# Values of two token chunks as one seven-product pair, with deadlines in the order model, in a tuned attention and feed-forward kernel

## The chip, the cores and the metric

The kernel runs on one core of a Trainium2 chip. The metric is the device time of that core in microseconds, the median of the timed runs. Runs of one version here lie up to 0.5% apart, so two versions are compared in rounds: both run by turns on the same chip. Where a **ratio** is given, it is the mean time of one kernel's fast runs over the mean of the other's in the same rounds, with a 95% interval; it is therefore not quite the ratio of the medians quoted beside it. One execution of each kernel is also recorded by the hardware profiler. All stage times below are from such traces.

## The reference

```python
x = A_x                                             # 2048 tokens x 1024, bf16
g = sigmoid((x * gate_w).sum(-1, keepdims=True))    # one gate for each token
a = attention(x, wqkv) @ wo                         # 32 heads, each token sees 8 tokens, 2 apart, itself included
b = (gelu(x @ w_gate) * (x @ w_up)) @ w_down        # inner width 3584
out = g * a + (1 - g) * b
```

The weights are `wqkv` (1024 x 3072), `wo` (1024 x 1024), `w_gate` and `w_up` (1024 x 3584) and `w_down` (3584 x 1024).

## The kernel before

The tokens are cut into four chunks of 512. Chunks 0 and 1 form a first pair, chunks 2 and 3 a second. The work of a pair is: projections to Q, K and V; up and gate products; down products, in which the attention output (with `wo`) and the feed-forward output (with `w_down`) are handled in one contraction.

Most of these products already use a **seven-product form**. A product of two matrices that are each cut into 2 x 2 quarters needs eight quarter products. Seven are enough if some of them take sums and differences of the quarters ("forms") as operands. TensorE saves one matmul in eight, and VectorE pays: it builds the forms of the weights and of x, and adds up partial results. In the kernel before, the up and gate products, the down products and the projections of chunks 2 and 3 are done so. The projections of chunks 0 and 1 are plain: for each chunk and each of Q, K and V, 8 output tiles x 8 contraction tiles = 64 matmuls of 128 x 512.

The order of instructions on every engine is fixed while the program is built. A small model holds a clock for each engine and a set of streams (generators of operations). It picks, again and again, the operation whose modelled start plus the bias of its stream is least:

```python
    def run(self, streams):
        ...
        while live:
            best = None
            for s in live:
                op = s[2] if isinstance(s[2], Op) else s[2]()
                t = None if op is None else self._start(op)
                if t is not None and (best is None or t + s[0] < best[0]):
                    best = (t + s[0], t, s, op)
            ...
            _, t, s, op = best
            self._emit(op, t)          # the engine order is now fixed
            s[2] = next(s[1], None)
    ...
    w.run([(0.0, main()), (0.0, loads()), (0.0, late_x()), (0.1, wforms()), (0.1, x_forms()), (0.1, qkv_forms()),
           (0.15, preps()), (0.3, attention()), (0.5, scores())])
```

`main` holds TensorE's work. `scores` and `attention` are the sliding-window attention on VectorE. `wforms` are the weight forms of up and gate. `preps` are the weight forms of the down products, prepared once and stored in DRAM: nine groups of four VectorE operations, each group loaded with 1 MB. The loads come in this order:

```python
    def loads():
        yield from load_qkv(0, 0)      # Q's weights, by eight rows of tiles, into ring buffers
        yield load_prep(0)
        yield from load_qkv(0, 1)      # K's
        yield Op("SP", ..., lambda: [nc.sync.dma_start(out=vbuf[...], in_=qkv_src(2, ...)) for hf in range(2)], ...)  # V's
        yield from load_x(1, [])
        yield load_prep(2)
        yield from load_block(0, 0)    # up and gate weights
        ...
    # main(), after the transposes of chunk 0
        yield from qkv_outer(0)        # Q of chunk 0
        yield from qkv(0, 1)
        yield from qkv(0, 2)           # V of chunk 0, 64 matmuls
        yield from gate(0)
        yield from halo(1)
        for which in range(3):
            yield from qkv(1, which)   # the third is V of chunk 1, 64 matmuls
            ...
        yield from gate(1)
```

Of the kernel before, what the change touches and what calls it, by code (L numbers as in the profile page):

```python
# [30 lines left out]
class Op:  # L31


    def __init__(self, eng, cost, fn, deps=(), key=None, table=None, pre=None, lag=0.0, tail=0.08, kind=None):
        self.eng, self.cost, self.fn, self.deps, self.key = eng, cost, fn, deps, key
        self.table, self.pre, self.lag, self.tail = table, pre, lag, tail
        self.kind = kind
        self.end = None


class Weave:
# [6 lines left out]
    RATE = 340e3  # L48

    def __init__(self, nc, tc):  # L50
        self.nc, self.tc = nc, tc
        self.clk = {e: 0.0 for e in ("PE", "DVE", "ACT", "POOL", "SP")}
        self.pipe = 0.0
        self.table = None
        self.done = {}
        self.last = {}
        self.log = []
        self.names = []

# [9 lines left out]
    def _start(self, op):  # L69
# [9 lines left out]
        t = self.clk[op.eng]  # L79
        for d in deps:  # L80
            t = max(t, d.end + (0.04 if d.eng == op.eng else self.LAT + op.lag))
        return t

    def _emit(self, op, t):
# [4 lines left out]
        if op.eng in ("SP", "POOL"):  # L89
            nbytes, issue = op.cost  # L90
            self.clk[op.eng] = t + issue
# [8 lines left out]
        for ins in self.nc.cur_bb.bb.instructions[n0:]:  # L100
# [4 lines left out]
            if prev is not None:  # L105
                self.tc.add_manual_dep(ins, prev, mybir.DependencyInfo(mybir.DependencyClass.NoSync,
                                                                      mybir.DependencyReason.DATA),
                                       reason="engine order")
            self.last[eng] = ins.name
# [5 lines left out]
    def run(self, streams):  # L115
# [5 lines left out]
        while live:  # L121
            best = None
            for s in live:
                op = s[2] if isinstance(s[2], Op) else s[2]()
                t = None if op is None else self._start(op)
                if t is not None and (best is None or t + s[0] < best[0]):
                    best = (t + s[0], t, s, op)
# [9 lines left out]
def kernel(  # L137
# [51 lines left out]
    hT = persist.tile([P, 2 * NST, FT, P], BF16)  # L189
# [8 lines left out]
    XB = 9  # L198
    ring = persist.tile([P, NG, GR], BF16)
# [3 lines left out]
    ident = hT[:, NST + 1, 0, :]  # L203
# [10 lines left out]
    def hflat(j, f0, n):  # L214
        return hT[:, j, f0:f0 + n, :].rearrange("p f s -> p (f s)")
# [57 lines left out]
    for j in range(NST):  # L273
        (nc.sync if j % 2 == 0 else nc.scalar).dma_start(out=hflat(j, 0, 8), in_=x[j * P:(j + 1) * P, :])
    warm = hT[:, NST, 0:SC // P, :].rearrange("p a b -> p (a b)")
# [19 lines left out]
    vbuf = hT[:, :, 0:NT, :].rearrange("p k f n -> p k (f n)")  # L295
    NPREP = FH + NTH
    NSTG = 3
    def stage(i):
        f0 = FT - 4 * (i + 1)
        return hT[:, :, f0:f0 + 4, :].rearrange("p (a b) f s -> p a b (f s)", b=2)  # L300
# [9 lines left out]
    def load_x(c, deps):  # L310
        deps = deps + ([[("acct", 1)], [("att", 0)]][c - 2] if c > 1 else [])
# [58 lines left out]
    def loads():  # L370
        yield from load_qkv(0, 0)
        yield load_prep(0)
        yield from load_qkv(0, 1)
# [3 lines left out]
        yield from load_x(1, [])  # L377
        yield load_prep(2)
# [7 lines left out]
        for sup in range(NSUP):  # L386
            c0 = 2 * sup
            more = sup + 1 < NSUP
            if more:
                yield from load_down(c0)  # L390
                for which in range(3):
                    yield from load_qkv(c0 + 2, which, [k for i in range(KH) for k in (i, i + KH)],
                                        [("wq", c0 + 2, which - 1, 3, KH - 1)] if which else [])
                yield from load_down(c0 + 1, [("wq", c0 + 2, 2, 3, KH - 1)])
# [6 lines left out]
    def preps():  # L401
        for i0 in range(0, NPREP, 2):
# [5 lines left out]
            f0 = dve(t, lambda: V(out=b11, in0=b12, in1=b11, op=ALU.subtract), [("prep", i0)], lag=1.0)  # L408
            yield f0
            yield dve(t, lambda: V(out=b12, in0=b22, in1=b12, op=ALU.subtract))  # L410
            f1 = dve(t, lambda: V(out=b22, in0=b22, in1=b11, op=ALU.subtract), [f0])
            yield f1
            last = dve(t, lambda: V(out=b21, in0=b21, in1=b22, op=ALU.subtract), [f1])
# [12 lines left out]
    def wforms():  # L426
        t = tt(GR)
        for b in range(NBLK):
            ops = []
            for f, x_, y_, op in ((0, "U21", "A22", ALU.add), (2, "A11", "U21", ALU.subtract), (1, 0, "A11", ALU.subtract),  # L430
# [5 lines left out]
                o = dve(t, go, [("w", 0, b, x_), ("w", 0, b, y_)], key=("w", 0, b, f), lag=0.5, pre=ring_pre)  # L436
# [28 lines left out]
    def qkv_w(c, which, kt):  # L465
        if c < 2 and which == 2:
            return vbuf[:, kt, :]
# [6 lines left out]
    def halo(c):  # L474
        for z, n in ((kT, 1), (vT, 2)):
            src = [("qkv", c - 1, n, t) for t in range(NT)]
            yield act(0.2, lambda z=z: nc.scalar.copy(out=z[c][:, :, 0:HALO], in_=z[c - 1][:, :, SC:SC + HALO]),
                      src + ([("acct", 2 * c - 3), ("att", c - 2)] if c > 2 else []),
                      key=("halo", c, n))

    def qkv(c, which):
        src = 0 if c < 2 else c
        shared = c < 2 and which == 2
        dw = [("wqkv", 0, 2)] if shared else [("wqkv", src, which, kt) for kt in range(KT)]
# [13 lines left out]
        if c != 0 and not shared:  # L498
            for kt in range(KT):
                ring_give(("wqkv", src, which, kt), o)  # L500

    def qkv_outer(c):
        taken = [bank_take() for t in range(NT)]
        for kt in range(KT):
# [11 lines left out]
            if c:  # L516
                ring_give(("wqkv", c, 0, kt), o)
# [10 lines left out]

    def qkv_forms():
        for sup in range(1, NSUP):  # L530
            c = 2 * sup
            t = tt(D // 2)
            for which in range(3):
                def g3(key):
                    return ring[:, held[key], :].rearrange("p (m t) -> p m t", t=NT)

                def raw(kt, hi, which=which, c=c):
                    return g3(("wqkv", c, which, kt))[:, :, KH * hi:KH * hi + KH]
# [5 lines left out]
                for f in range(4):  # L544
                    for kt in range(KH):
                        if True:
# [9 lines left out]
                            dep = [("wqkv", c, which, kt), ("wqkv", c, which, kt + KH)]  # L556
                            if f in (1, 2):
                                dep.append(("wq", c, which, 0, kt))
                            elif f == 3:
                                dep.append(("wq", c, which, 1, kt))  # L560
                            yield dve(t, go, dep, key=("wq", c, which, f, kt), lag=0.5,
                                      pre=ring_pre if (f != 2 and kt % 2 == 0) else None)

    def q_tmp(t):
        return hT[:, t // 2, FT - NT + KH * (t % 2):FT - NT + KH * (t % 2 + 1), :].rearrange("p f s -> p (f s)")

    def v_tmp(t):
        v = hT[:, t, FH:FH + KH, :] if t < 2 else hT[:, 2 + (t - 2) // 3, NTH + KH * ((t - 2) % 3):NTH + KH * ((t - 2) % 3 + 1), :]
        return v.rearrange("p f s -> p (f s)")

    def v_move(c):
# [3 lines left out]
        def fn():  # L575
            nc.sync.dma_start(out=dst[:, 0:2], in_=hT[:, 0:2, FH:FH + KH, :].rearrange("p j f s -> p j (f s)"))
            for j in range(2):
                nc.sync.dma_start(out=dst[:, 2 + 3 * j:5 + 3 * j],
# [711 lines left out]
```

## Time and profile before

| | |
|---|---|
| median of 4 timed runs | 730.04 us (729.64 to 730.49) |
| the profiled execution | 728.63 us, so 1 us faster than any of the timed ones |
| matmuls | 3397 |

The first part of the page of the kernel before gives busy time, share of the span and number of instructions for each engine:

```profile
PE 721.2 (99%) x3397; PEld 355.8 (49%) x3397; DVE 593.9 (82%) x874; ACT 316.0 (43%) x533; POOL 72.4 (10%) x128
```

The second part cuts the span into 40 slices of 18 us; each digit is the busy share in tenths. VectorE (DVE) is at nine tenths or more in most slices to 260 us:

```profile
DVE  2769999999999989986999979989999995793200
DMA  9985868998887969964128999857576656999992
```

The chain of waits of the kernel before, in order of time, shows what the end time hangs on. The columns are the start, the length (us), then engine, tile, line and number of instructions. L472 are the plain projections, L973 the up and gate products, L608 the seven-product projections of chunks 2 and 3:

```profile
49.90 13.97 PE ps L472 x64
...
64.05 27.78 PE ps L472 x128
...
92.37 5.30 PE ps L973 x24
...
97.84 63.99 PE ps L973 x296
...
161.85 97.76 PE ps L973 x452
...
317.57 72.67 PE ps L608 x336
```

The last line gives the price of a matmul in a dense stream: 72.67 us / 336 = 216.3 ns.

PE's waits in the kernel before are tiny. The columns are the tile, the line, what it waited for, then total us, how often, longest:

```profile
PE ps L278 <- DVE hT L276: 1.2, 1, 1.2
PE ps L1215 <- DMA hT<-in_A_x_dram: 0.6, 1, 0.6
PE ps L472 <- DVE lend L1222: 0.2, 1, 0.2
```

All three are at the start, before or in the first projections. There is also a table of stretches of the same kernel. After the length come the busy time and count of each engine, then TensorE's clock, the DMA share (the mean busy share of the core's 16 DMA engines; the view can show a little over 1) and GB/s.

```profile
core 0: us, PE busy (x) PEld busy (x) DVE busy (x) ACT busy (x) POOL busy (x), PEclk, DMA share, GB/s
92.37:130.00 37.63, 37.63 (x183) 16.98 (x183) 36.73 (x60) 22.03 (x39) 13.17 (x21) 1.00 0.78 252
130.00:165.00 35.00, 34.98 (x163) 15.79 (x162) 32.48 (x50) 21.91 (x37) 12.91 (x21) 1.00 1.08 350
```

From 92 to 130 us VectorE is busy for 36.73 of 37.63 us (98%), and from 130 to 165 us the DMA share is at its top, 1.08 at 350 GB/s. TensorE is not the only engine without slack there.

### The profile page before, as it was taken

The page shows a single profiled execution, that of the slowest core. Times are in us where ns is not written, and L with a number is a line of the kernel's source. Part 1 is how long each engine was busy: PE and PEld are TensorE (multiplying, and loading weights), DVE is VectorE, ACT ScalarE, POOL GpSimd, SP SyncE. Part 2 cuts the span into 40 slices and gives each one's busy share as a digit, 9 for nine tenths or more (in the row PEclk, how much of TensorE's full clock was granted, in tenths as well). Part 3 has the DMA queues.
Part 4 walks back from the last instruction along what each step waited for, and adds up shares of the span by engine and source line. Part 5 has one row for each costly group of instructions (what it writes and reads, how often), then busy time and mean ns, then how long its engine had stood idle before and what let it go on. Part 6 is the DMA issues. An engine that isn't in the chain of part 4 may idle for free.

```text
span 726.9 us, 9989 instructions
## 1 busy us (share of the span) xinstructions
PE 721.2 (99%) x3397; PEld 355.8 (49%) x3397; DVE 593.9 (82%) x874; ACT 316.0 (43%) x533; POOL 72.4 (10%) x128
## 2 busy tenths in 40 slices
PE   8999999999999999999999999999999999999998
PEld 6666644444444444456665444444444444444443
DVE  2769999999999989986999979989999995793200
ACT  2333455576555561045443114585558556210110
POOL 1131224443212000000000000000000000001000
PEclk9999999999999999999999999999999999999999
DMA  9985868998887969964128999857576656999992
GB/s 305 273 264 157 236 209 293 319 367 274 214 215 203 232 197 339 329 193 128 47 87 282 353 315 358 250 156 183 149 184 160 173 150 171 306 333 333 328 308 99
DMA packets 185043, 172.12 MB, mean 237 GB/s; under 512 B 56480, under 2 KB 145568, under 8 KB 184992
## 3 DMA queue, kind: packets, MB, share of 16 engines
q1 hardware_dynamic: 176160, 143.69, 67.7%
q0 software_dynamic: 8544, 27.27, 10.2%
q8 instruction: 26, 0.43, 0.2%
q10 hardware_dynamic: 288, 0.52, 0.2%
q14 instruction: 25, 0.20, 0.1%
HBM read 129.50 MB, written 28.31 MB: 217 GB/s over the span
## 4 chain that ended last, share of the span: by engine, by line
PE 98%; ACT 1%; DMA 0%; issue 0%; DVE 0%; ACTq 0%
PE ps L973 46%; PE ps L1120 30%; PE ps L472 11%; PE ps L608 10%; DMA hT<-in_A_x_dram 0%; PE ps L1215 0%; PE ps L716 0%; ACT L1061 0%; ACT L882 0%; ACT ost L1155 0%; ACT gl L1061 0%; PE ps L740 0%; ACT xbuf L883 0%; ACT m L1027 0%; ACT ps L1002 0%
## 5 line engine op out<-in xcount | busy, mean ns | idle before, releaser
L973 PEld LDWEIGHTS <-ring 128*128 128x128 bf16 x1568 | 153.2, 98 | 185.5 <-issue 1.3
L973 PE MATMUL ps<-lend,ring 128*128 128x512 bf16 x896 | 212.3, 379 | 0.1
L973 PE MATMUL ps<-tf,ring 128*128 128x512 bf16 x672 | 164.0, 379 | 0.0
L1120 PE MATMUL ps<-ring,hT 128*128 128x512 bf16 x708 | 160.6, 379 | 0.0
L1120 PEld LDWEIGHTS <-hT 128*128 128x128 bf16 x708 | 69.2, 98 | 83.3
L925 DVE TENSOR_TENSOR xbuf<-xbuf,lend 128x2048 bf16<-128x2048 bf16 x64 | 77.4, 1216 | 2.5 <-DMA xbuf<-xbuf 2.5
L779 DVE TENSOR_TENSOR xbuf<-qo,lend 128x2048 bf16<-128x2048 bf16 x64 | 77.1, 1217 | 2.2 <-ACT lend L494 2.1
L785 DVE TENSOR_TENSOR xbuf<-xbuf 128x2048 bf16<-128x2048 bf16 x56 | 68.1, 1217 | 0.2
L1155 ACT ACTIVATE ost<-ps,omg 128x512 bf16<-128x512 f32 x16 | 11.0, 688 | 113.7 <-PE ps L1120 113.7
L608 PEld LDWEIGHTS <-ring 128*128 128x128 bf16 x336 | 43.9, 131 | 28.9 <-DMA xbuf<-xbuf 0.4
L1002 ACT COPY ps<-ps 128x512 f32<-128x512 f32 x56 | 32.0, 571 | 56.3 <-PE ps L973 56.2
L472 PE MATMUL ps<-lend,ring 128*128 128x512 bf16 x256 | 55.9, 379 | 0.2 <-DVE lend L1222 0.2
L1045 ACT ACTIVATE gl<-ps 128x512 bf16<-128x512 f32 x56 | 33.5, 598 | 50.8 <-PE ps L973 49.8
L1147 POOL DMA_DIRECT2D out_dram<-ost x24 | 13.0, 542 | 422.1 <-ACT ost L1155 331.7
L1017 DVE TENSOR_TENSOR hT<-hT,gl 128x1024 bf16<-128x1024 bf16 x56 | 38.5, 688 | 13.4 <-ACT hT L1014 12.2
L1120 PE MATMUL ps<-ring,qo 128*128 128x512 bf16 x192 | 49.3, 379 | 0.0
L1057 DVE TENSOR_TENSOR u<-ps,u 128x512 f32<-128x512 f32 x56 | 38.5, 687 | 9.2 <-PE ps L973 8.3
L472 PEld LDWEIGHTS <-ring 128*128 128x128 bf16 x256 | 36.8, 144 | 18.6 <-issue 0.7
L608 PE MATMUL ps<-lend,ring 128*128 128x512 bf16 x192 | 43.5, 379 | 0.0
L442 POOL DMA_DIRECT2D fforms<-ring x56 | 30.7, 548 | 119.6 <-DVE ring L434 110.7
L933 DVE TENSOR_TENSOR xbuf<-xbuf 128x1024 bf16<-128x1024 bf16 x64 | 41.8, 685 | 0.6
L1036 DVE TENSOR_TENSOR hT<-ps,m 128x512 bf16<-128x512 f32 x56 | 38.4, 686 | 4.8 <-PE ps L973 4.4
(103 smaller groups left out, 684.4 us busy)
## 6 DMA issues: line engine op xcount, KB each, us to landing
ring<-dforms SPq DMA_DIRECT2D x112, 256.0 KB, 5.0
ring<-in_B_w_down_dram SPq DMA_DIRECT2D x84, 256.0 KB, 4.3
ring<-in_B_w_gate_dram SPq DMA_DIRECT2D x56, 256.0 KB, 5.0
fforms<-ring POOLq DMA_DIRECT2D x56, 256.0 KB, 5.0
ring<-fforms SPq DMA_DIRECT2D x56, 256.0 KB, 4.0
ring<-in_B_w_up_dram SPq DMA_DIRECT2D x42, 256.0 KB, 3.8
ring<-in_A_wqkv_dram SPq DMA_DIRECT2D x40, 256.0 KB, 5.5
ring<-oforms SPq DMA_DIRECT2D x32, 256.0 KB, 5.5
```

Source lines behind the costliest of these rows:

```text
L472: nc.tensor.matmul(banks[bk][:], lhsT=lhsT, rhs=xT(c, kt), start=(kt == 0), stop=(kt == KT - 1))
L608: nc.tensor.matmul(banks[bk][:], lhsT=lhsT, rhs=rhs[:, kt, :], start=(start and kt == 0), stop=(kt == KH - 1), skip_group_check=True)
L779: V(out=w3(box[t]), in0=q_b, in1=k_w, op=ALU.mult)
L785: V(out=w3(box[0]), in0=w3(box[0]), in1=w3(box[t]), op=ALU.add)
L925: return dve(tt(n), taking(("p", t), lambda: V(out=w3(box["p", t]), in0=w3(box["ab"]), in1=v_w, op=ALU.mult)), [("qkv", c, 2, t), abo] + ( ...
L933: V(out=s4(t)[:, t % 2], in0=w3(box["p", t])[:, 0:4], in1=w3(box["p", t])[:, 4:8], op=ALU.add)
L973: nc.tensor.matmul(banks[bk][:], lhsT=wv[:, k, fl * P:(fl + 1) * P], rhs=rhs[:, k, :], start=(start and k == 0), stop=(k == KH - 1), skip_ ...
L1017: yield dve(tt(2 * SC), lambda f=f: nc.vector.tensor_tensor(out=hT[:, :, f, :], in0=hT[:, :, f, :], in1=gl[f][:].rearrange("p (j s) -> p j ...
L1036: ev[f, "up2"] = dve(tt(SC, True), lambda f=f: nc.vector.tensor_tensor(out=hs(f, 1), in0=v3(banks[Bk[f]][:]), in1=v3(m5[f][:]), op=ALU.add ...
L1045: nc.scalar.activation(out=gl[f][:, SC:2 * SC], in_=banks[A[f]][:], func=ACT.Gelu_apprx_tanh)
L1057: e = dve(tt(SC, True), lambda f=f: nc.vector.tensor_tensor(out=u2[f][:], in0=banks[Dk[f]][:], in1=u2[f][:], op=ALU.add), [o, ev[f, "u2"]])
L1120: nc.tensor.matmul(banks[bk][:], lhsT=l, rhs=wv[:, i, :], start=(start and k == 0), stop=(q == last and i == 1), skip_group_check=True)
```

## The change

Intent: V of chunks 0 and 1 in one seven-product pair. Seven products of 4 output tiles x 4 contraction tiles are 112 matmuls in place of 128. To make room for VectorE's additional work (16 weight forms and 8 sums), the order is re-tuned:

- The first preparation of down weights is loaded after x of chunk 1. Its VectorE work and that of later groups gets a deadline. A stream's bias holds an operation back until the modelled time comes within 11 us of its deadline; then the bias drops to zero.
- The down forms become a stream of their own, split by feed-forward part and attention part, so that the feed-forward part need not wait for attention.
- The big buffer `hT` is laid out with the other axis first, so that Q's and V's weights can lie in it in whole rows. (The transposed order of layout has no effect on what is computed.)

The diff also makes the second pair take V before K (`QVK`) and moves a few waits between scores, attention and loads; these are left out here. The core of the diff, with cuts:

```diff
@@ the order model
-                if t is not None and (best is None or t + s[0] < best[0]):
-                    best = (t + s[0], t, s, op)
+                if t is None:
+                    continue
+                b = s[0] if op.due is None or t + self.AHEAD < op.due else 0.0      # AHEAD = 11.0
+                if best is None or t + b < best[0]:
+                    best = (t + b, t, s, op)
...
-    hT = persist.tile([P, 2 * NST, FT, P], BF16)
+    hT = persist.tile([P, FT, 2 * NST, P], BF16)
+    hrow = hT[:].rearrange("p f j s -> p f (j s)")
+    DUE = (88.5, 308.0)
...
-    vbuf = hT[:, :, 0:NT, :].rearrange("p k f n -> p k (f n)")
+    vbuf = hrow[:, 0:KT, :]
+    qbuf = hrow[:, KT:2 * KT, :]
...
     def loads():
-        yield from load_qkv(0, 0)
-        yield load_prep(0)
-        yield from load_qkv(0, 1)
+        for kt in range(KT):
+            yield Op("SP", (P * D * 2, 0.45), lambda kt=kt: nc.sync.dma_start(
+                out=qbuf[:, kt:kt + 1], in_=qkv_src(0, kt, 1)), key=("wqkv", 0, 0, kt))
+        yield from load_qkv(0, 1, range(KT))
         yield Op("SP", ...)          # V's weights
         yield from load_x(1, [])
+        yield load_prep(0)
         yield load_prep(2)
...                                  # preps: each of the four operations of a group
-            f0 = dve(t, lambda: V(out=b11, in0=b12, in1=b11, op=ALU.subtract), [("prep", i0)], lag=1.0)
+            f0 = dve(t, lambda: V(out=b11, in0=b12, in1=b11, op=ALU.subtract), due=DUE[0] + 4.0 * i0, deps=[("prep", i0), ], lag=1.0)
...                                  # wforms
+                        due=DUE[0] + 12.1 * b)
...
     def qkv_forms():
-        for sup in range(1, NSUP):
+        for sup in range(NSUP):
...
-            for which in range(3):
+            for which in QVK if sup else (2,):                                       # QVK = (0, 2, 1)
...
+    def down_forms():
+        for c in range(NCH):
...
+            def ready(g, part):
+                home = [("pr", c - 1, 6, 1)] if c % 2 else [("att", c, 1)] if c else []
+                return [("ffn", c // 2), ("att", c, g) if part else ("h", c // 2, FT - 1)] + home
...
     def main():
         yield from qkv_outer(0)
         yield from qkv(0, 1)
-        yield from qkv(0, 2)
         yield from gate(0)
+        yield from qkv_pair(0, [2])
+        yield from gate_sum(0)
+        yield from qkv(1, 0)
+        yield from qkv(1, 1)
+        yield from gate(1)
         yield from halo(1)
-        for which in range(3):
-            yield from qkv(1, which)
-            if which == 0:
-                yield from gate_sum(0)
-        yield from gate(1)
...
-    w.run([(0.0, main()), (0.0, loads()), (0.0, late_x()), (0.1, wforms()), (0.1, x_forms()), (0.1, qkv_forms()), (0.15, preps()), (0.3, attention()), (0.5, scores())])
+    w.run([(0.0, main()), (0.0, loads()), (0.0, late_x()), (0.88, wforms()), (0.0, down_forms()), (0.1, x_forms()), (1.43, qkv_forms()),
+           (1.3, preps()), (0.13, attention()), (0.36, scores())])
```

## The prediction

> **What bounds the kernel.** TensorE, in every stage. The page's first part has PE busy 721.2 of 726.9 us (99%), and the chain of waits is PE for 98%. Its idle time is at the ends: some 2 us before the first matmuls, and 3.6 us after the last (one ScalarE scaling and the store). A table by stretches shows PE idle 0.02 us in 92 to 260, none in 260 to 445, 0.12 in 445 to 612. VectorE is next: 593.9 us (82%), 95% in 92 to 260, but PE hardly waits for it. So only fewer matmuls, or a new stall, can move the time.
>
> **Cost of a matmul.** The profile prints 379 ns for a 128x512 matmul, but they overlap: in the chain of waits 336 take 72.67 us, 216.3 ns each. The Trainium skill ("TensorE: Matmul & The Clock Gate", Back-to-back issue gap) gives N/2.4 + 2.5 = 216 ns for an isolated one and 131 ns sustained; this trace shows 216 sustained.
>
> **What changes.**
> - PE: V of chunks 0 and 1 was 2x8x8 = 128 matmuls; seven half-size products are 112. The instruction order shows 16 fewer matmuls in all. 16 x 0.2163 = 3.46 us, all on the critical path.
> - VectorE: 16 weight-form operations (417 ns in the later pairs, about 0.34 us back to back) and 8 PSUM additions (0.69 us): about 11 us more, at 25 to 60 us. It idled about 8 us in 20 to 60; the rest is found by putting preparations of the down weights later.
> - ScalarE: 20 evacuations where 16 were, +2.4 us, on an engine at 43%.
> - DMA: the same bytes. Q's weights go to a free part of hT, and the first 1 MB preparation comes after x of chunk 1.
> - Deadlines, and down forms split by h and attention part: the same VectorE work (each form was two instructions already) in another order. No gain by themselves; they pay for the extra VectorE work.
>
> **Can it stall?** The V pair starts at 35.9 us and needs x of chunk 1 14 us sooner than x was needed. Before, T1 began at 34.4 us; with 1 MB less ahead of it, at about 300 GB/s, that is some 3 us sooner. V's weights should land near 25 us, their forms end by 31, T1 and T2 by 34, against need at 37.7 and 39.4; T3 near 38.5 against 42. The up/gate phase starts about 88.9 us with VectorE nearly full: the tightest place, slack 1 to 2 us. These are estimates from durations in the trace.
>
> **Prediction.** 730.13 - 3.46 = 726.67; with a little for small new waits **726.8 us**, range 725.9 to 728.4. Faster by over 2%: 0.01; within 2%: 0.97; slower by over 2%: 0.02.
>
> **What would show it.** PE with 3381 matmuls, busy about 717.7 us, span about 723.5; the first up/gate product at 88.9 us instead of 92.4; every later stage as long as before; VectorE busy about 605 us; no entry over 0.3 us in PE's waits.
>
> **What would make it wrong.** PE waiting for T1, T3 or V forms at 36 to 48 us, for the first up/gate weight forms at 89 to 100 us, or for attention or down forms at 255 to 275 or 387 to 395 us. VectorE has about 5% slack there; a stall could eat 1 to 3 us, the whole gain. A gain above 4 us would mean that something besides matmul count bound the kernel.

## The result, and the profile after

| | before | after |
|---|---|---|
| median of 4 runs | 730.04 us (729.64 to 730.49) | 725.69 us (725.55 to 725.79) |
| ratio, same rounds | | 0.994 [0.9923, 0.9957] |

The gain is 730.04 - 725.69 = 4.35 us. The forecast was a gain near 3.3 us; the result lies 0.2 us below the forecast's range. The size class (within 2%) is as forecast.

The first two parts of the page after:

```profile
PE 713.6 (99%) x3314; PEld 351.1 (49%) x3381; DVE 598.5 (83%) x898; ACT 315.3 (44%) x535; POOL 71.8 (10%) x128
...
DVE  1799999999999899799599976999999995794200
DMA  9944799989989979945239999786566657999992
```

TensorE's count is to be read from the weight loads (PEld): 3381, 16 fewer than before. Of the matmul records themselves 67 are missing from this trace, so PE's busy time (713.6) must not be set against the 721.2 of before.

PE's waits after:

```profile
PE ps L298 <- DVE hT L296: 1.2, 1, 1.2
PE ps L1252 <- DMA hT<-in_A_x_dram: 0.5, 1, 0.5
PE ps L628 <- DVE lend L481: 0.5, 1, 0.5
PE ps L995 <- ACT m L1049: 0.4, 1, 0.4
PE ps L496 <- DVE lend L1259: 0.3, 1, 0.3
```

There are two waits that before did not have: 0.5 us for the third form of x of the second pair (L481, at 320 us) and 0.4 us for ScalarE's part of the gelu (L1049, at 175 us). The chain of waits after, near 320 us, shows the first: VectorE makes the fourth row of weight forms (L576), then the x form, and only then can the projection products (L628) go on:

```profile
318.72 1.34 DVE ring L576 x4
320.06 1.15 DVE lend L481
321.21 0.05 issue
321.25 6.91 PE ps L628 x31
```

The timeline after (start, length, engine, line, operation, out<-in) shows that the pair itself started as forecast: T1, the first form of x, at 30.3 us, and the pair's first product at 35.3 us:

```profile
30.33 1.21 DVE L477 TENSOR_TENSOR tf<-lend,lend 128x2048 bf16<-128x2048 bf16 x1
...
35.29 1.95 PE L628 MATMUL ps<-lend,hT 128*128 128x512 bf16 x8
```

The stretches after:

```profile
88.11:130.00 41.89, 41.59 (x201) 18.96 (x202) 41.42 (x65) 24.48 (x45) 15.90 (x26) 1.00 1.00 333
130.00:165.00 35.00, 34.84 (x161) 15.85 (x162) 34.72 (x54) 19.43 (x35) 14.02 (x22) 1.00 0.92 290
```

VectorE is now busy for 41.42 of 41.89 us (99%) and the DMA load is spread (1.00 and 0.92 in place of 0.78 and 1.08). The change did not make VectorE less busy. It is fuller, and TensorE still hardly waits for it.

A table of stages, from the start of the first weight load of each in the trace (us). "Start" ends at the first projection product. The first row is the one trace that was there for the forecast; the next three are further traces of the very same kernel, taken in the experiments:

| kernel, trace | start | projections 0/1 | up/gate, pair 1 | sum of the three | down 0 | projections 2/3 | end of the last matmul |
|---|---|---|---|---|---|---|---|
| before, first | 7.36 | 84.94 | 166.94 | 259.24 | 58.26 | 72.91 | 723.25 |
| before, e1 | 7.55 | 85.97 | 167.10 | 260.62 | 58.26 | 72.91 | 724.63 |
| before, e7 | 7.67 | 85.59 | 167.41 | 260.67 | 58.26 | 72.91 | 724.68 |
| before, e8 | 6.52 | 85.86 | 168.25 | 260.63 | 58.26 | 72.91 | 724.64 |
| after, first | 6.52 | 81.60 | 167.25 | 255.37 | 58.26 | 73.63 | 720.08 |
| after, e4 | 7.11 | 81.44 | 167.22 | 255.77 | 58.26 | 73.07 | 719.92 |

The later stages (down 1: 54.19, up/gate of pair 2: 166.9, down 2 and 3: 111.75) are the same in all of them. Two things stand out. The first trace of before is 1.4 us shorter than the other three. And those three agree to 0.05 us on the end of the third stage, although their first two stages add up to 93.52, 93.26 and 92.38 us. Something other than TensorE seems to pin that end. But the waits are small, and the 1.4 us do not arise in one place: at the end of the projections e1 and e7 are already 1.22 and 0.96 us behind the first trace (92.30 us), and e8, level with it there, loses 1.31 us in up/gate.

### The profile page after: what moved, and what is told of

The parts are those of the page before. It is cut to its first block, busy times and chain, and to the rows that moved or that the text cites. A ratio compares the mean times of both kernels' runs of the same rounds, so it can differ in the third digit from the quotient of the medians.

```text
span 723.8 us, 9915 instructions
## 1 busy us (share of the span) xinstructions
PE 713.6 (99%) x3314; PEld 351.1 (49%) x3381; DVE 598.5 (83%) x898; ACT 315.3 (44%) x535; POOL 71.8 (10%) x128
## 4 chain that ended last, share of the span: by engine, by line
PE 83%; DVE 8%; DMA 4%; issue 4%; POOL 1%; ACT 0%; DVEq 0%; POOLq 0%; ACTq 0%
PE ps L995 35%; PE ps L1159 28%; PE ps L628 12%; PE ps L496 8%; DMA fforms<-ring 1%; DVE ring L457 1%; DVE ring L576 1%; DVE hT L1058 1%; DMA ring<-in_B_w_down_dram 1%; DMA ring<-in_A_wqkv_dram 1%; DMA hT<-in_A_wo_dram 1%; DMA hT<-in_B_w_down_dram 1%; DVE hT L1120 1%; DVE hT L1039 1%; DVE hT L433 0%
## 5 line engine op out<-in xcount | busy, mean ns | idle before, releaser
L995 PEld LDWEIGHTS <-ring 128*128 128x128 bf16 x1568 | 153.2, 98 | 185.8 <-issue 1.6
L995 PE MATMUL ps<-lend,ring 128*128 128x512 bf16 x877 | 210.5, 379 | 1.3 <-ACT m L1049 0.4
L995 PE MATMUL ps<-tf,ring 128*128 128x512 bf16 x659 | 162.6, 379 | 0.7
L804 DVE TENSOR_TENSOR xbuf<-xbuf 128x2048 bf16<-128x2048 bf16 x56 | 68.2, 1217 | 0.3
L628 PEld LDWEIGHTS <-ring 128*128 128x128 bf16 x384 | 49.3, 129 | 34.4 <-DVE lend L481 0.9
L466 POOL DMA_DIRECT2D fforms<-ring x56 | 30.6, 546 | 175.3 <-DVE ring L457 166.1
L628 PE MATMUL ps<-lend,ring 128*128 128x512 bf16 x203 | 47.0, 380 | 0.7 <-DVE lend L481 0.5
L628 PE MATMUL ps<-tf,ring 128*128 128x512 bf16 x173 | 40.1, 379 | 0.2
L1075 ACT COPY u<-ps 128x512 f32<-128x512 f32 x56 | 32.9, 587 | 15.1 <-PE ps L995 15.1
```

Source lines behind the costliest of these rows:

```text
L628: nc.tensor.matmul(banks[bk][:], lhsT=lhsT, rhs=rhs[:, kt, :], start=(start and kt == 0), stop=(kt == KH - 1), skip_group_check=True)
L804: V(out=w3(box[0]), in0=w3(box[0]), in1=w3(box[t]), op=ALU.add)
L995: nc.tensor.matmul(banks[bk][:], lhsT=wv[:, k, fl * P:(fl + 1) * P], rhs=rhs[:, k, :], start=(start and k == 0), stop=(k == KH - 1), skip_ ...
```

## The experiments

Two theories were set against each other. **Count:** TensorE alone bounds the kernel; 16 matmuls less give 3.46 us wherever they are taken out, and the rest of the gain is chance at the start: when x lands, and when TensorE is granted its full clock (in the trace of e1 the first projection products start 427 ns apart, and 216 ns apart from about 10.1 us on). **Order:** in the first 165 us VectorE and DMA are as much the limit as TensorE; matmuls taken out there are handed back as waits unless VectorE's order is changed as well, and the new order also takes out waits that ordinary executions of before have.

### e1, e7, e8: before again; e4: after again

No edit.

> The kernel before, unchanged. The measured gain was 4.35 us by the medians, but the two profiled executions differ by only 3.1 us (726.9 to 723.8), because the profiled execution of before took 728.6 us where its timed ones took 729.6 to 730.5. Theory 'unsteady before': before loses 1 to 2 us in some executions, in stalls that its first trace does not show; then its times here spread over 728.6 to 730.5 us and this new trace may show a gap of TensorE of 0.5 to 2 us somewhere between the first projection and the last product. Theory 'steady': all agree within 0.3 us and the second trace is like the first.

> The changed kernel, unchanged, beside the others on one chip. Expected 725.6 to 725.8 us, 4.3 us under before if before is at 730.0 us. Theory 'unsteady before': the changed kernel spreads by less than 0.4 us, and the gain over the fastest executions of before is about 3.1 us.

> The kernel before once more, for another trace. Under 'clock grant' its time is 727.9 us plus what the late grant costs (0.7 us at 7.4, 1.9 us at 10.1 us); every stage after 50 us is as long as in the other two traces. Under 'late stalls' a stage after 50 us is longer by 0.5 us or more when the time is over 730 us.

> As the run before this one: a fourth trace of the kernel before, to see which stage carries the difference between its executions.

Measured: e1 729.99 us (6 runs, 728.77 to 731.36), ratio 1.0002 [0.9984, 1.0021]. e7 730.06 and e8 730.05, one run each. e4 725.49 (725.16 to 725.87), ratio 0.9942 [0.9927, 0.9958]. So the result repeats. The kernel before spreads over some 4 us from run to run (728.5 to 732.7 over all rounds), the kernel after over less than 1 us.

The traces e7 and e8 show what the first trace hid. The chain of waits of e7 leaves PE at 160 us, for an up weight that lands at 165.03 us. The 4.79 us are the chain's last piece of that load, not a wait; the product itself waited 0.4 us for it.

```profile
98.80 61.42 PE ps L973 x284
160.22 0.02 issue
160.24 4.79 DMA ring<-in_B_w_up_dram
165.03 0.03 issue
```

The chain of e8 leaves PE for VectorE and ScalarE at 99.8 us (and again, for a gate weight that ends at 163 us):

```profile
97.93 1.85 PE ps L973 x8
...
99.80 0.68 DVE xbuf L933
100.48 0.61 DVE u L1057
...
101.11 0.63 ACT gl L1061
101.74 0.48 ACT m L1027
...
151.67 11.29 DMA ring<-in_B_w_gate_dram
```

In all three further traces the next run of products starts at 165.02 to 165.06 us. PE's waits over 0.2 us in this stage add up to 0.4 us in e7 and 1.1 us in e8; e1 has none, though its chain too runs through an up weight that lands at 165.02 us. The first trace went through at 161.85 us without waiting, after a start that was also among the best: it was a lucky execution.

### e2: the pair alone

The pair is put into the kernel before, with its old layout, biases and forms. Q's weights must lie in the big buffer, in the old layout:

```diff
+    qbuf = hT[:, :, NT:2 * NT, :].rearrange("p k f n -> p k (f n)")
...
-        yield from load_qkv(0, 0)
-        yield load_prep(0)
+        for kt in range(KT):
+            yield Op("SP", ..., lambda kt=kt: nc.sync.dma_start(out=qbuf[:, kt:kt + 1], in_=qkv_src(0, kt, 1)), ...)
...
+        yield from qkv_pair(0, [2])    # in main(), as in the change
```

> The kernel before with the seven-product V pair alone (Q's weights in hT, the first preparation after x of chunk 1, which the pair needs); no deadlines, old biases, old down forms, old layout of hT. Theory 'matmul count': 16 matmuls less, 3.46 us under before (about 726.6 us), plus any stall that the untuned order brings: trace with 3381 weight loads. Theory 'the order pays for the pair': VectorE's 11 us more meet an order that does not expect them, TensorE stalls 1 to 4 us, and the time is 727 to 730 us. If it is as fast as the full change (4.3 us under before), the deadlines and the split are worth nothing.

Measured: 747.01 us (746.29 to 747.36), ratio 1.0235 [1.0216, 1.0255]: slower by 17 us. PE's waits:

```profile
PE ps L475 <- DMA hT<-in_A_wqkv_dram: 8.8, 1, 8.8
PE ps L1121 <- DVE hT L1089: 4.9, 1, 4.9
```

The first wait has a cause that neither theory held. In the old layout Q's rows and V's rows lie interleaved in `hT`. In the trace, the first weight load of Q's fifth row waits on two semaphores: that of its own load, which landed at 10.8 us, and that of V's weights. The second half of V was issued at 14.3 us and landed at 23.7 us. In the new layout the two lie in separate rows, and the wait is gone. So the layout, which looks like tidying, spares the pair this wait of 8.8 us. The second wait is for a down form. The pair alone gains nothing; but as this kernel also carries the layout trouble, it says little of VectorE by itself.

### e3: the order without the pair

The kernel after, with V of chunks 0 and 1 plain again:

```diff
-            for which in QVK if sup else (2,):
+            for which in QVK if sup else ():
...
         yield from qkv(0, 1)
+        yield from qkv(0, 2)
         yield from gate(0)
-        yield from qkv_pair(0, [2])
-        yield from gate_sum(0)
         yield from qkv(1, 0)
+        yield from gate_sum(0)
         yield from qkv(1, 1)
+        yield from qkv(1, 2)
```

> The changed kernel with V of chunks 0 and 1 as plain products again (128 matmuls), all else of the change kept: deadlines, split down forms, layout, load order. Theory 'matmul count only': equal to before within 0.3 us (730.0 us) . Theory 'the order is worth the missing 0.9 us': about 0.9 us under before (729.1 us).

Measured: 734.69 us (732.85 to 736.73), ratio 1.0069 [1.0048, 1.009], slower by 5 us. PE's longest wait here is for the third x form of the second pair:

```profile
PE ps L628 <- DVE lend L481: 3.7, 1, 3.7
```

Neither theory foresaw this loss. A likely reading, not tested, is that the deadlines are tuned to a modelled clock: with plain V everything runs 3.5 us later against fixed deadlines, and an operation that was just in time is late. The order "by itself" gives nothing, as forecast, and even loses; an order tuned again for plain V was not tried.

### e5, e6: two more warm-up matmuls

With five dummy matmuls, the full clock of TensorE was granted anywhere from 5.2 to 10.2 us in the traces. Two more keep TensorE busy until x lands:

```diff
-    for i in range(5):
+    for i in range(7):
         nc.tensor.matmul(banks[7][:], lhsT=warm[:, 0:P], rhs=warm, start=True, stop=True)
```

> The kernel before with seven warm-up products instead of five, so that TensorE is busy until x lands (the five end at about 3.5 us, x lands at 4.04 to 4.29 us). Two profiled executions of before differ by 1.4 us, 1.2 of it before 50 us: the full clock was granted at 7.4 us in one and at 10.1 us in the other, and the first products ran at 427 ns meanwhile. Theory 'clock grant': the idle gap before x decides when the clock is granted; with seven the trace shows the grant before 7.5 us, the slow executions go, the times lie within 1 us and the median is 0.8 to 1.5 us under before. Theory 'late stalls': the spread of before (728.5 to 732.3 us) stays, since its cause lies later.

> The changed kernel with seven warm-up products. Theory 'clock grant': its grant is early already (5.6 and 6.5 us in two traces), so it gains at most 0.3 us and its distance to the warm before shrinks to the 3.5 us of the 16 matmuls. Theory 'late stalls': the distance stays at 4 us or more.

Measured: on before 729.54 us, ratio 0.9998 [0.9984, 1.0011]; on after 725.43 us, ratio to before 0.9939 [0.9925, 0.9952], as without the edit. In the trace of e5 the clock came at 6.8 us and the projections took 84.61 us in place of the 85.59 us that four traces of before average; the time of the six runs did not follow. In e6 the clock came at 4.4 us. So seven dummy matmuls bring nothing that can be seen. This does not rule out that chance at the start is part of the extra gain: the interval of e5 reaches from 1.2 us faster to 0.8 us slower, and when the clock came in the five runs without a trace is not known. In the traced execution of e5 itself the good start was kept (up/gate 167.17 us, 728.92 us in all); in e8 one of the same size was lost again.

### e9, e10: the load order alone

```diff
# e9: before                               # e10: after
         yield from load_qkv(0, 0)                  out=qbuf[...], ...
-        yield load_prep(0)                +        yield load_prep(0)
         yield from load_qkv(0, 1)                  yield from load_qkv(0, 1, range(KT))
...                                        ...
         yield from load_x(1, [])                   yield from load_x(1, [])
+        yield load_prep(0)                -        yield load_prep(0)
```

> The kernel before with one move: the first 1 MB preparation of the down weights is loaded after x of chunk 1 instead of between Q's and K's weights (the change does the same). Five traces of before differ only in the first 170 us: projections 84.6 to 86.0 us, first up/gate phase 166.9 to 168.3 us, in waits for Q's and K's weights, for the late clock and for a late VectorE. Theory 'load order': that 1 MB makes the weights late and VectorE with them; then the median is 1.0 to 1.5 us under before (about 728.4 us) and the times lie within 1 us. Theory 'VectorE's order': the load order alone changes less than 0.4 us, the waits at 101 and 164 us stay, and the spread stays near 3 us.

> The changed kernel with that preparation back between Q's and K's weights. Theory 'load order': K's weights and x of chunk 1 are late again, the V pair waits for them, and 1 to 3 us of the gain go, with a spread over 1.5 us. Otherwise 725.5 us as the changed kernel.

Measured: e9 736.95 us, ratio 1.0086 [1.0069, 1.0104]: slower by 6.3 us. e10 728.7 us, ratio to before 0.9976 [0.9962, 0.999]. On the chip of e9 to e12 the kernel before itself ran at 730.65 us, about 1 us slower than in the rounds of e4. So these runs are set against the kernel after by their distance to before in the same rounds: e10 is 1.8 us faster than before where after is 4.35 us faster (e4), hence 2.5 us slower than after. PE's waits in e9:

```profile
PE ps L973 <- ACT m L1027: 3.2, 2, 1.7
PE ps L973 <- DVE hT L1036: 1.3, 1, 1.3
```

A moved load makes the model plan VectorE anew, and with the old biases the new plan is bad; neither theory foresaw a loss. The theory "the later load alone brings the extra gain" falls. Each half also needs the other: the tuned order with the old load order loses more than half of the gain.

### e11: no deadlines

The kernel after with the old biases and no deadlines:

```diff
-                b = s[0] if op.due is None or t + self.AHEAD < op.due else 0.0
+                b = s[0]
...
-    w.run([... (0.88, wforms()), (0.0, down_forms()), (0.1, x_forms()), (1.43, qkv_forms()), (1.3, preps()), (0.13, attention()), (0.36, scores())])
+    w.run([... (0.1, wforms()), (0.0, down_forms()), (0.1, x_forms()), (0.1, qkv_forms()), (0.15, preps()), (0.3, attention()), (0.5, scores())])
```

> The changed kernel with its deadlines taken out and the stream priorities of before put back; V pair, layout of hT, load order and split down forms stay. Theory 'the deadlines pay for the pair': VectorE does weight forms and preparations too early, attention and x forms come late, TensorE stalls 2 to 8 us at the first up/gate phase, at the chunk 2/3 projections or at the down products, and the time is 728 to 734 us. If it stays within 0.5 us of 725.5, the deadlines are worth nothing.

Measured: 741.4 us (4 fast runs), ratio 1.0142 [1.0123, 1.016]; by the distances to before, 15 us above the kernel after. PE's waits:

```profile
PE ps L1159 <- DVE qo L962: 5.2, 2, 3.9
PE ps L628 <- DVE ring L576: 2.5, 1, 2.5
```

The waits are for the end of attention before the down products (near 400 us) and for weight forms (at 320 us). The first up/gate stage, where the waits were expected, took 166.71 us and was fine.

### e12: down forms joined again

```diff
-                return [("ffn", c // 2), ("att", c, g) if part else ("h", c // 2, FT - 1)] + home
+                return [("ffn", c // 2), ("att", c, 1), ("h", c // 2, FT - 1)] + home
...                                  # and the products wait for both parts
```

> The changed kernel with its down forms and down products waiting again for all of h and both attention halves of their chunk together; all else as changed. Theory 'the split is slack only': within 0.3 us of 725.5 us, since attention is done before the down products start. Theory 'the split pays': TensorE stalls 0.5 to 5 us at the down products of an odd chunk (383 to 395 us), as in the trace of the pair alone, which waited 4.9 us for a down form there.

Measured: 728.19 us, ratio to before 0.9965 [0.9951, 0.998]; by the distances to before, 1.8 us above the kernel after. PE's waits:

```profile
PE ps L995 <- ACT m L1049: 2.4, 5, 0.8
```

The five waits lie in the second up/gate stage (450 to 561 us), not at the down products: once more the edit's own place is fine, and the replanned order loses elsewhere.

### e13, e14: lighter preparation loads (wrong results on purpose)

The last six preparations are loaded for 8 of 128 partitions, to lighten DMA from 90 us on:

```diff
+                m = P if i0 < 2 * NSTG else 8
                 for k in range(n):
-                    nc.sync.dma_start(out=st[:, 2 * h + k], in_=v[:, k])
+                    nc.sync.dma_start(out=st[0:m, 2 * h + k], in_=v[0:m, k])
```

> The kernel before with the last six preparations loaded for 8 of 128 partitions only (5.6 MB less to load between 60 and 170 us; a wrong result on purpose; every instruction in its old place). Theory 'DMA paces before at 165 us': that wait goes, the first down product starts at or under 259.4 us, the median falls by 0.8 to 1.5 us to about 728.6 us and the spread to under 1.5 us. Theory 'chance at the start': nothing changes by more than 0.3 us.

> The changed kernel with the same loads cut (wrong on purpose). Theory 'DMA paces before only': within 0.3 us of the changed kernel, about 725.4 us, so that the distance to the lightened before is 3.1 to 3.6 us, the 16 matmuls. Otherwise the changed kernel gains as much as before did and the distance stays at 4 us or more.

Measured: e13 729.35 us, ratio 0.9988 [0.9975, 1.0]: 0.5 to 0.9 us faster than before, hardly separated from it. e14 725.37 us, ratio to before 0.9939 [0.9927, 0.995], as the kernel after. The DMA load matters little, if at all, and only before. The 16 matmuls were not left out together with a lighter DMA load.

### e15: 16 matmuls left out of before (wrong result)

This is the count by itself. One of the eight contraction steps of V is left out in both chunks. The order of the other instructions is the same on every engine:

```diff
-        nc.tensor.matmul(banks[bk][:], lhsT=lhsT, rhs=xT(c, kt), start=(kt == 0), stop=(kt == KT - 1))
+        nc.tensor.matmul(banks[bk][:], lhsT=lhsT, rhs=xT(c, kt), start=(kt == 0), stop=(kt == KT - 1 - (c < 2 and which == 2)))
...
-                for kt in range(KT):
+                for kt in range(KT - shared):
```

> The kernel before with 16 of its 128 matmuls for V of chunks 0 and 1 left out (one of eight along the contraction; wrong on purpose) and every other instruction in its old place: the count alone. Theory 'count': 3.4 to 3.5 us under before, 726.1 to 726.3 us. Theory 'DMA paces before at 165 us': part of that is given back in waits for up and gate weights between 100 and 170 us, and the gain is 1 to 3 us.

Measured: 729.83 us (728.10 to 732.45), ratio 0.9999 [0.9982, 1.0015]. **Sixteen matmuls less gave nothing that can be seen**; by the interval at most 1.3 us, where the count asks for 3.46. The projections took 81.60 us, as short as after, but up and gate took 171.47 us in place of 166.94 to 168.25. PE's waits:

```profile
PE ps L973 <- ACT m L1027: 2.1, 1, 2.1
...
PE ps L740 <- DVE zq L726: 1.0, 1, 1.0
PE ps L973 <- DVE hT L1036: 0.9, 2, 0.7
```

The stretches of e15:

```profile
88.88:130.00 41.12, 38.08 (x183) 17.08 (x184) 40.53 (x65) 21.79 (x39) 14.81 (x24) 1.00 0.81 264
130.00:165.00 35.00, 33.99 (x157) 15.20 (x156) 31.06 (x49) 21.43 (x36) 12.81 (x21) 1.00 1.09 332
```

PE is idle for 3.0 us from 88.9 to 130 us and 1.0 us to 165 us, while VectorE is busy for 40.53 of 41.12 us. One operation of VectorE tells it most plainly, the sum `u` of the first up/gate block. The timeline of before, and then that of e15:

```profile
98.78 0.68 DVE L1057 TENSOR_TENSOR u<-ps,u 128x512 f32<-128x512 f32 x1
```

```profile
99.15 0.68 DVE L1057 TENSOR_TENSOR u<-ps,u 128x512 f32<-128x512 f32 x1
```

TensorE came 3.5 us earlier, yet VectorE reached this operation 0.4 us later than before. Its own earlier work had not become less: in both traces four preparation operations of 0.7 us each run between 92.5 and 96.5 us, ahead of `u`. (The `ACT m` that PE waits for is the step behind `u`, as in the chain of e8: `u`, `gl`, `m`.)

### e16: the third x form first

```diff
-    w.run([... (0.1, x_forms()), ...])
+    w.run([... (-0.5, x_forms()), ...])
```

> The changed kernel with the forms of x put ahead of other VectorE work in the order model. The wait of 0.1 to 0.7 us for the third form of x at 320 us should go: 725.0 to 725.5 us if nothing else is disturbed; slower than 725.7 us if what it displaces is waited for instead.

Measured: 725.56 us, ratio to before 0.9936 [0.9924, 0.9948]. The wait at 320 us is gone (that stage takes 72.91 us as before), but the time is that of the kernel after.

### e17, e18: lighter VectorE work, without and with the 16 matmuls (wrong results on purpose)

If VectorE is the limit, cutting its work must make the missing matmuls count. The VectorE operations of the last six preparations work on 8 of 512 columns; the loads stay. e17 is before with this edit, e18 is e15 with it:

```diff
             fo = (b11, b22, b12, b21)
+            if i0 >= 2 * NSTG:
+                b11, b12, b21, b22 = [z[:, :, 0:8] for z in fo[0:1] + fo[2:4] + fo[1:2]]
```

> The kernel before with the VectorE work of the last six preparations cut (24 operations of 0.6 us, about 14 us of VectorE between 92 and 165 us; wrong on purpose; same instructions in the same places, same loads and stores). Theory 'VectorE paces before up to 165 us': the waits at 101 and 164 us go, 728.0 to 729.0 us, a spread under 2 us. Theory 'DMA paces it': no change from before.

> The same with the 16 matmuls of V left out as well. Theory 'VectorE paces before': the 16 matmuls now count, 2.5 to 3.5 us under the run before this one, 724.7 to 726.2 us. Theory 'something else gives it back': equal to the run before this one within 1 us.

Measured: e17, five fast runs, mean 728.58 us, ratio 0.9984 [0.9971, 0.9997]. e18, six runs, mean 726.05 us, ratio 0.995 [0.9937, 0.9962]. So with lighter VectorE work the 16 matmuls are worth 728.58 - 726.05 = 2.53 us; without it they were worth 0 (e15). The stretches of e18, to be set against those of e15:

```profile
88.88:130.00 41.12, 40.72 (x202) 18.24 (x195) 36.64 (x68) 23.31 (x41) 15.01 (x24) 1.00 0.84 283
130.00:165.00 35.00, 34.98 (x163) 15.78 (x162) 28.23 (x55) 22.24 (x38) 15.29 (x24) 1.00 1.08 352
```

PE is idle for 0.4 us where it was idle for 3.0. DMA is as full as in e15 (1.08 against 1.09), and PE hardly waits any more (0.4 us for ScalarE's `m`). The sum `u`, at 99.15 us in e15, now comes 2.4 us sooner, since the four preparation operations ahead of it take 0.16 to 0.17 us each:

```profile
96.75 0.68 DVE L1059 TENSOR_TENSOR u<-ps,u 128x512 f32<-128x512 f32 x1
```

That separates VectorE from DMA.

The profiled execution of e17 is no evidence: it took 2730.56 us. Its matmuls start 840 ns apart, nearly four times the usual. The other five runs were normal, and they alone are used.

## Why the prediction was right or wrong

**Right.**
- 16 matmuls fewer (3397 to 3381), 216.3 ns each, 3.46 us off the projections. The projections fell from 85.59 us (mean of four traces) to 81.52 us (mean of two).
- The pair was not late. The first x form of the pair started at 30.3 us and the second was done by 32.7 (forecast: both by 34), and the first up/gate product at 88.1 us (forecast 88.9).
- Later stages kept their length, 58.26, 54.19, 166.9 and 111.75 us, but for the projections of chunks 2 and 3, which grew by 0.2 to 0.7 us.
- VectorE has 24 operations more (874 to 898). Added up one by one, VectorE's operations take 642.6 us before and 653.6 us after: the 11 us more that were forecast. The busy time, in which overlapping records count once, rose only to 598.5 us (forecast "about 605"); the pair in the old order has 603.9 us (e2).
- "A gain above 4 us would mean that something besides matmul count bound the kernel." That is what came.

**The step that failed: "TensorE, in every stage", "PE hardly waits for it", "So only fewer matmuls, or a new stall, can move the time".** This rested on PE being 99% busy, on a chain that is PE for 98%, and on one trace. That trace was among the fastest executions of before (728.63 us; all its runs lie from 728.45 to 732.68 us), and its up/gate stage has no wait over 0.2 us where e7 and e8 have 0.4 and 1.1 us. With it falls "16 x 0.2163 = 3.46 us, all on the critical path": in the old order the 16 matmuls are worth 0 us (e15). e17 with e18 shows what was missing: with 24 VectorE operations made light, before gains 0.16% (some 1.2 us, interval 0.2 to 2.1) with its matmul count unchanged, and the 16 matmuls are then worth 2.53 us. In the first 165 us VectorE bounds the kernel before as much as TensorE. The Trainium skill ("Perfetto Trace Analysis", Identifying the Most-Contended Engine) warns that a matmul's busy share is a poor measure of how close a kernel is to its limit; this case agrees, with 99% busy and 0 us for 16 matmuls. That the forecast still came within 1.1 us of the result is in part luck: in the old order the matmuls that it counted would not have paid.

**Wrong in its wording: "No gain by themselves; they pay for the extra VectorE work".** The first half holds (e3 loses 5 us). But the order seems to pay for more than the additional 24 operations. Without it even the bare saving of matmuls, with no additional VectorE work, gives nothing (e15). Without deadlines the pair ends 15 us above the kernel after (e11), with early preparations 2.5 us above (e10), with joined forms 1.8 us above (e12).

**Mis-sized: "730.13 - 3.46 = 726.67; with a little for small new waits 726.8".** The new waits (0.5 us at 320 us, 0.4 us at 175 us) are over the 0.3 us that the forecast allowed and not at the places that it listed. The larger error is the base. 730.13 us is the median of the timed runs that were there, 1.5 us above the traced execution (728.63 us) whose waits were analysed, and the forecast takes its whole length, what it loses beyond the matmuls included, over into the kernel after. From the traced execution the sum comes out: 728.63 - 3.46 + 0.44 (projections 2/3, read afterwards) = 725.61 us; measured, 725.69 us. Where the rest lies shows in the sum of the stages, mean of four traces of before against two of after: start -0.46, projections -4.07 (3.46 of it by count), up/gate -0.19, projections 2/3 +0.44; together -4.28 us, of which -0.82 is not count. In timed runs it is 4.35 - 3.46 = 0.9 us. Little of this surplus is in up/gate. 0.78 us are won by the end of Q and K of chunk 0 (35.74 us before, 34.96 after, means of the same traces), ahead of all that the pair changes on TensorE; from there to up/gate every trace of before takes 57.13 us and every one of after 53.37, which is 0.30 us beyond the count; together with the -0.19 and the +0.44 this nearly cancels. The e17 figure of 1.2 us is of the same size as the surplus, but that does not show that the two are the same time.

**How the new order makes room** can in part be read from the traces, though no run isolates it. Here is VectorE's busy time (us), added up from the traces by the part of the program that a line belongs to. The stretches are counted from the first up/gate product of each kernel (92.37, 88.88 and 88.11 us). "Attention" is its second part, after the scores; "up/gate's own" is the `u` sums, the products with gelu and the like. (Single operations overlap a little, so parts can add up to more than the stretch.)

| | before | e15 | after |
|---|---|---|---|
| attention, up to the first up/gate product | 11.2 | 8.2 | 5.9 |
| attention, next 22 us | 9.8 | 12.9 | 5.8 |
| attention, next 62 us | 9.6 | 9.2 | 16.6 |
| attention, sum of the three | 30.6 | 30.3 | 28.3 |
| up/gate's own, next 22 us | 5.5 | 4.1 | 5.5 |

All three do about the same attention work in the end. In the order of before, 21 us of it stand ahead of the 22-us mark. When TensorE arrives 3.5 us sooner (e15), what VectorE has not finished is pushed into the opening of the up/gate stage (12.9 us in place of 9.8), and the stage's own operations, which TensorE needs, come late (4.1 us in place of 5.5). After has only 11.7 us of attention ahead of that mark, in spite of the work for the pair, and moves the rest to where the stage has run in. It is the order of VectorE's work and not its amount: after does more of it. This reading fits e15 and e8 (`u` and the gelu steps are what is late), but it is read from traces and not tested by a run of its own. Attention as such is not the cause: e18 has as much of it in those 22 us as e15 and still 5.5 us of the stage's own work, since its preparations take about 1 us there in place of 3. What counts is VectorE's total in that stretch.

**Still open.** The cause of the additional 0.8 us, and its split among a better start, weight waits near 165 us and VectorE. The start may not be chance alone: TensorE begins on x by 4.18 us in eight of nine traces with the new layout, and in three of ten with the old one (e17 left out). No run tests this. The lighter DMA of e13 brought 0.5 to 0.9 us, the lighter VectorE of e17 1.2 us, with intervals that overlap; and e5 shows only that two more dummy matmuls bring no gain in before. No run was clearly faster than the kernel after: e6 (725.43), e14 (725.37, wrong result) and e16 (725.56) are within its spread.

## What to carry to other kernels

Where a second engine is at 98% behind a first at 99%, the first is not "the" bound: leave the saved instructions out of the old kernel (results wrong, order unchanged) and see whether the time falls, before building the version that saves them properly. Take several traces of the kernel before as well; one profiled execution that is faster than every timed run is a hint that its waits are not the usual ones. In a kernel whose order a model fixes, a saving and the order tuned for it work only together: here each part alone gave from nothing to 17 us of loss.

## What the Trainium skill lacked or had wrong

- "TensorE: Matmul & The Clock Gate", Back-to-back issue gap: it gives 216 ns for an isolated 512-column matmul and about 131 ns for a sustained stream of weight loads and matmuls. The densest stream here, 336 matmuls in 72.67 us, runs at 216.3 ns each; 131 ns is seen nowhere, and the 216 ns that this section calls isolated are what the sustained stream takes.
- The same page, What's actually happening: it says that the moment of the full clock varies by 500 ns to either side. In the traces with five dummy matmuls the grant came from 5.2 to 10.2 us; with seven, which leave hardly a gap ahead of x, it came at 6.8 us (e5) and 4.4 us (e6). With five: where x landed by 4.13 us it came by 7.4 us; where x landed at 4.22 us or later, it came at 6.9 to 10.2 us. On average the late landings have the grant 2.5 us later (8.8 against 6.3 us); whether TensorE's idle gap ahead of x is the cause stays open (e5 and e6 close it, with one trace each).
- The same page, Part 4: PE-mode transpose: it says that the full clock does not engage for transposes. In the trace of the kernel after, transposes start 107 ns apart before the grant at 5.61 us and 56 ns apart after it. Whether they help to earn it is not shown, as five ordinary matmuls run ahead of them.
- The same page, Seeing it yourself: it says that clock events in the trace are unreliable and that a quarter clock was seen for over 50 us. Here one execution (e17's first) ran for the whole 2730 us with matmuls 840 ns apart, while the trace records the full clock.
- "VectorE: DVE Perf Modes", The perf-mode tier table, is confirmed: 1224 ns for a bf16 sum of 2048 columns, 1217 ns in the trace of before.
- No page that was consulted says that a row-interleaved buffer can tie two loads together: in e2 a weight load waited 8.8 us for another tensor's DMA, since the two lay interleaved in one tile.
